# Keys and queries of one token tile as one unit of 1216 columns over three PSUM banks

## The chip, the cores and the metric

The kernel runs on one core of one Trainium2 chip. The metric is the device time of one execution in microseconds. A PSUM bank holds 512 fp32 columns for each of 128 partitions; the core has eight, numbered 0 to 7. The engines are TensorE (PE, with its weight loads as a lane of their own, PEld), VectorE (DVE), ScalarE (ACT), GpSimd (POOL) and SyncE (SP, which issues DMAs here).

## The reference

The input x has 2048 tokens of 640 features, in bf16. Two branches are mixed by a gate g = sigmoid(sum(x * gate_w)) per token:

```python
a = attention(x)                                   # 32 heads of 20
b = (gelu(x @ w_gate) * (x @ w_up)) @ w_down       # 1728 hidden columns
return g * a + (1 - g) * b
```

The attention is linear. With q, k, v = x @ wqkv, each head of q and k goes through a 20 x 20 matrix `w_phi`, and its features are softmax(p) and softmax(-p) side by side (40 of them). Then kv = phi_k^T v and z = sum of phi_k over all tokens, and each token gets phi_q kv / (phi_q z + 1e-6), followed by `@ wo`.

## The kernel before

Matmuls take a 128-token tile of x (transposed, `xT`, five blocks of 128 features) as the stationary operand and stream weights, so each projection of a tile is a group of five matmuls that accumulate in one bank, once for each feature block `kt`. Early on, `fold` multiplies `w_phi` into the K and Q weights and subtracts the last feature of each head, so that a head needs 19 columns: K and Q have 32 x 19 = 608 columns each, `wk2` inside the weight tile `w3` (beside V's 640 columns and the gate's one) and `wq2` in a tile of its own.

608 columns do not fit a bank. `k_tile` and `q_tile` each use a pair of banks and split the columns 304 and 304, so that the result lies contiguous over the border of the two banks: it begins at column `KO` = 208 of the first. `v_tile` does the same with 345 and 296 (`VO` = 167; 641 columns with the gate's). One ACT instruction then reads across the border: `exps` makes two of them for K or Q, exp(p) and exp(-p), into `Ek` or `Eqt`; V is copied into `vaug`. `exps` reads 33 heads in 11 groups of three, 627 columns, so the 19 columns behind the 608 must be zero; `strip` clears them in each second bank once. `gate_exp` handles the gate column (`gcol`), which comes with V, or with K for tiles 0 to 3 and 5.

The scheduler `_Sched` writes instructions in the program's order on each engine and tracks hazards by bank: a matmul into a bank waits for all that have read the bank before. The order is written out by hand in `attention_state`. K tiles 0 to 3 and V tiles 0 to 8 are done before the projection loop. The loop has 16 steps `s`, in turns of four by r = s % 4:

- r other than 1: `k_tile` of the next K tile (4 to 15) in banks 2 and 3, and `k_norm` on DVE (sums, reciprocal, scaling of `Ek`)
- s above 0 and r other than 0: `gram`, 11 matmuls (line 602) that add one K tile and its V to the state, which stays in banks 4 and 5
- s above 0 and r of 0 or 1: `v_tile` of the next V tile (9 to 15) in banks 0 and 1
- every step: `q_tile` of tile s in banks 6 and 7, and an SP transpose of `Eqt` into `Eq`
- every step above 0: one piece of the gate and up weights loaded on SP

Behind the loop `ffn` runs the gate and up projections (512-column matmuls), with the last four grams between them, then numerators (line 760) and the down and output projections (line 815).

All projections are recorded by the helper `mm` at line 459, so they share that line; shapes and operands tell them apart (`wq` is Q's weight before). `exps` is line 530, V's copy 500, the gate's exponential 520, the K normalisation lines 582, 590 and 591.

Of the kernel before, what the change touches and what calls it, by code (L numbers as in the profile page):

```python
# [3 lines left out]
P = 128  # L4
BF16 = mybir.dt.bfloat16
F32 = mybir.dt.float32
# [101 lines left out]
class _Kernel:  # L108
    S, D, H, DH, F = 2048, 640, 32, 20, 1728
    KD = D // P  # L110
# [16 lines left out]
    HG = 3  # L127
    UP = (4, 5, 6)
    LATE = (2, 3)
    VO = 167  # L130
    KO = 208

    def __init__(self, nc, A_x, A_wqkv, A_w_phi, A_wo, B_x, B_w_gate, B_w_up, B_w_down, gate_w, out):
        self.nc = nc
# [14 lines left out]
    def alloc(self):  # L149
        nc = self.nc  # L150
        S, D, KD, NT, BT, NFC, DH = self.S, self.D, self.KD, self.NT, self.BT, self.NFC, self.DH
        T = nc.alloc_sbuf_tensor
        self.xT = T("xT", [P, KD, S], BF16)
        self.wo_sb = T("wo_sb", [P, KD, D], BF16)
        self.wg_sb = T("wg_sb", [P, KD, 13 * P], BF16)
        self.wu_sb = T("wu_sb", [P, KD, 13 * P], BF16)
        self.wgu_sb = T("wgu_sb", [P, KD, P], BF16)
        self.wd_sb = T("wd_sb", [P, NFC, D], BF16)
        self.Eq = T("Eq", [P, self.G, S], BF16)
        self.KV = T("KV", [P, self.G, self.HG * self.DB], BF16)  # L160
        self.hmask = T("hmask", [P, 3, self.HG], BF16)
        self.mask = T("mask", [P, KD, 8], BF16)
        self.ident = T("ident", [P, P], BF16)
        self.gz = T("gz", [P, P], BF16)
        self.gcol = T("gcol", [P, NT], F32)
        self.gtmp = T("gtmp", [P, NT], F32)
        self.Gm = T("Gm", [P, NT], F32)
        self.Gr = T("Gr", [P, NT], F32)
        self.BD = T("BD", [P, KD, 8 * DH], BF16)
        self.wref = T("wref", [P, KD, self.H], F32)  # L170
        self.wphi_sb = T("wphi_sb", [P, KD, DH], BF16)

        def place(lists):
            size = {"b": 0}
            plans = []
            for items in lists:
                c = 0
                for name, shape, dt in items:
                    n = mybir.dt.size(dt)
                    for s_ in shape[1:]:  # L180
                        n *= s_
                    c = (c + 31) // 32 * 32
                    plans.append((name, shape, dt, c))
                    c += n
                size["b"] = max(size["b"], c)
            arena = T("arena%d" % len(self._arenas), [P, size["b"]], mybir.dt.uint8)
            self._arenas.append(arena)
            base = nc.lookup_mloc(arena).addr
            for name, shape, dt, c in plans:
                setattr(self, name, nc.alloc_sbuf_tensor_at(name, shape, dt, offset=base + c))  # L190
        self._arenas = []
        place([
            [("w3", [P, KD, D + 2 + self.H * self.E], BF16)],
            [("hT0", [P, NFC, BT], BF16), ("gl", [P, 3, BT], BF16)],
        ])
        place([
            [("Ek", [P, self.NSE, self.G * P], BF16), ("vaug", [P, self.NSV, self.H, self.DA], BF16)],
            [("hT1", [P, NFC, BT], BF16)],
        ])
        place([  # L200
            [("Eqt", [P, self.NEQ, self.G * P], BF16), ("Dk", [P, self.NSE, 2, 2 * self.G * self.HG], F32)],
            [("hT2", [P, NFC, BT], BF16)],
        ])
        place([
            [("wkT", [P, KD, D], BF16), ("wqT", [P, KD, D], BF16), ("wq2", [P, KD, self.H * self.E], BF16),
             ("xtok", [P, self.TB, D], BF16)],
            [("ahead", [P, 2 * KD, D], BF16), ("kstage", [P, self.HM * DH], F32)],
            [("upl", [P, len(self.LATE), BT], F32), ("qstage", [P, self.HM * DH], F32)],
            [("under", [P, KD, 2 * D + self.H * self.E], BF16), ("upf", [P, len(self.UP), BT], F32)],
            [("goT", [P, 8, KD, P], BF16), ("O1", [P, 2, D], BF16), ("O2", [P, 2, D], BF16),  # L210
             ("Og", [P, 2, D], BF16), ("RH", [P, 2, 8, self.H], F32), ("outsb", [P, 4, D], BF16)],
        ])
        self.ps = nc.alloc_psum_tensor("ps", [P, 4096], F32)
# [167 lines left out]
    def fold(self, name, main, tail, evacs, clear=None):  # L381
# [16 lines left out]
        for _, r, b, top, bot, (kt, i, k0, c, n) in sorted(order, key=lambda o: o[:2]):  # L398
            a, opens = 64 * r, opener.setdefault(b, r) == r
# [8 lines left out]
        for what, x in evacs:  # L408
            if what == "strip":
                self.strip(x)  # L410
            elif what == "tail":
                self.fold_evac(name, (0, 3)[x], (3, 2)[x], tail[x], self.HM, self.H)
            else:
                self.fold_evac(name, x, 1, main[x], 0, self.HM)

    def folded(self, name, kt, n, h0, w):
        T, c = (self.w3, self.D + 1) if name == "k" else (self.wq2, 0)
        c += h0 * self.E
        return T[:, kt:kt + n, c:c + w * self.E].rearrange("p k (h f) -> p k h f", f=self.E)

    def fold_evac(self, name, kt, n, b, h0, h1):
        w = h1 - h0
# [22 lines left out]
            dst, src[:, :, 0:self.E], src[:, :, self.E].unsqueeze(2).to_broadcast([P, self.HM, self.E]), ALU.subtract),  # L445
            reads=[key], writes=[("w%s2" % name, kt)])

    def strip(self, b, ek="d"):

        c = (b + 1) * 512 + 304  # L450
        dst, wr = self.ps[:, c:c + self.E], [("ps", b + 1)]
        if ek == "d":
            self.sc.op("dve", lambda e: e.memset(dst, 0.0), writes=wr)
        else:
            zero = self.nc.const_aps.tensor(0.0, [P, self.E], F32)
            self.sc.op("act", lambda e: e.activation(dst, zero, AF.Copy), writes=wr)
# [63 lines left out]
        self.sc.op("act", lambda e: e.activation(self.gcol[:, t:t + 1], self.ps[:, c:c + 1], AF.Exp, scale=-1.0),  # L520
                   reads=[("ps", b)], writes=[("gcol", t)])

    def exps(self, T, sl, name, b):

        o = b * 512 + self.KO
        src = self.ps[:, o:o + self.G * self.HG * self.E].rearrange("p (g h f) -> p g h f", h=self.HG, f=self.E)
        for s, scale in ((0, 1.0), (1, -1.0)):
            dst = T[:, sl, :].rearrange("p (g s w) -> p s g w", s=2, w=64)[:, s, :, 0:self.HG * self.DH].rearrange(
# [9 lines left out]
    def up_ahead(self, j, b, ek):  # L538
# [9 lines left out]
        else:  # L548
            self.sc.op("act", lambda e: e.activation(out, self.bank(b), AF.Copy), reads=[("ps", b)], writes=[("upf", c)],
                       guard=old)  # L550

    def k_tile(self, t, b):
        g = 1 if t < self.TB or t == 5 else 0
        n = 512 - self.KO + g
        self.proj(t, self.D + 1 - g, n, b, self.KO - g, ["wk2"] + ["wgate"] * g)
        self.proj(t, self.D + 1 - g + n, self.H * self.E + g - n, b + 1, 0, ["wk2", "wk2t"])
        self.exps(self.Ek, t % self.NSE, "Ek", b)
        if g:
            self.gate_exp(t, b, b * 512 + self.KO - 1)

    def q_tile(self, t, b):
        n = 512 - self.KO
        for bk, c0, a, z in ((b, self.KO, 0, n), (b + 1, 0, n, self.H * self.E)):
            for kt in range(self.KD):
                self.mm(bk, c0, z - a, self.xT[:, kt, t * P:(t + 1) * P], self.wq2[:, kt, a:z], kt == 0,
                        kt == self.KD - 1, [("xT", t), ("wq2", kt), ("wq2t", kt)])
        sl = t % self.NEQ
        self.exps(self.Eqt, sl, "Eqt", b)
        self.sc.dma("sp", lambda e: e.dma_start_transpose(self.Eq[:, :, t * P:(t + 1) * P], self.Eqt[:, sl, :]),
                    reads=[("Eqt", sl, 0), ("Eqt", sl, 1), ("Eqtc", sl), ("Eqtp", sl)], writes=[("Eq", t)])  # L570

    def k_view(self, se):
        v = self.Ek[:, se, :].rearrange("p (u w) -> p u w", w=64)[:, :, 0:self.HG * self.DH]
# [22 lines left out]
    def gram(self, t):  # L596
        se, sv = t % self.NSE, t % self.NSV
        w = self.HG * self.DA
        va = self.vaug[:, sv, :, :].rearrange("p h c -> p (h c)")
        for g in range(self.G):  # L600
            n, b, c = min(w, self.H * self.DA - w * g), 4 + g // 8, w * (g % 8)
            self.sc.op("pe", lambda e: e.matmul(  # L602
                self.bank(b)[:, c:c + n], self.Ek[:, se, g * P:(g + 1) * P], va[:, w * g:w * g + n],
                start=(t == 0 and g in (0, 8)), stop=(t == self.NT - 1 and g in (7, 10)), skip_group_check=True),
# [5 lines left out]
    def kv_state(self):  # L610

        sc = self.sc
        m = self.hmask[:, 2, :]
        for b, g0, n, h in ((4, 0, 8, 3), (5, 8, 2, 3), (5, 10, 1, 2)):
            c = (g0 % 8) * self.HG * self.DA
            src = self.bank(b)[:, c:c + n * h * self.DA].rearrange("p (g h c) -> p g h c", h=h, c=self.DA)
            dst = self.KV[:, g0:g0 + n, 0:h * self.DB].rearrange("p g (h c) -> p g h c", c=self.DB)[:, :, :, 0:self.DA]
# [17 lines left out]
    def attention_state(self):  # L635
# [20 lines left out]
        for t in range(4):  # L656
            vs(t, 4)
            ve([t], "ad"[t % 2], False)
            if t == 2:
# [13 lines left out]
        self.up_ahead(3, 0, "a")  # L673
        self.up_ahead(4, 2, "a")
        self.k_sums(0)
        self.fold("q", (4, 5, 0, 3, 1), (6, 7), [(m, 0), (m, 1), (p, 4), (m, 2), (m, 4), (p, 0), (t, 0), (t, 1), (p, 6)],
                  2)
        k(1, 2)
        k(2, 4)
        k(3, 0)  # L680
        v(8, 6)
        self.k_scale(0)
        for t in range(1, 4):
            self.k_norm(t)
        nk, nv, ng = 4, 9, 0
        pieces = self.gate_pieces()
        for s in range(NT):
            r = s % 4
            if r != 1:
                k(nk, 2)  # L690
                self.k_norm(nk)
                nk += 1
            if s and r != 0:
                self.gram(ng)
                ng += 1
            if s and r in (0, 1):
                v(nv, 0)
                nv += 1
            q(s, 6)
            if s:  # L700
                pieces.pop(0)()
        for p in pieces:
# [46 lines left out]
    def num(self, t):  # L749
        sc = self.sc  # L750
        NBK = self.NUMB
        DB, DH, H = self.DB, self.DH, self.H
        old = [("upf", c) for c in self.UP + self.LATE] + ["kstage", "qstage"] + [("wq2t", k) for k in range(5)] + [("xtok", k) for k in range(4)] + ["wkT", "wqT"] + [("wq2", k) for k in range(5)]
        w = self.HG * DB
        base = [(NBK + 2 * s) * 512 + 512 - 6 * w for s in (0, 1)]
        for g in range(self.G):
# [8 lines left out]
        sl = t % 2  # L765
# [28 lines left out]
    def down_pair(self, t0, banks, widths):  # L794
# [66 lines left out]
        (w, k) for w in ("vaug", "vmain", "vone") for k in range(9)]  # L861
    oldq = [("Eqt", k, s) for k in range(4) for s in (0, 1)] + [(w, k) for w in ("Eqtc", "Eqtp") for k in range(4)] + [
        (w, k) for w in ("Dk", "Rk") for k in range(5)]
    oldw = [(w, k) for w in ("wv", "wk2", "wk2t") for k in range(5)] + ["wgate"]

    def ffn(self):
        self.gn = 0
# [83 lines left out]
```

## Time and profile before

| | us |
|---|---|
| median of 3 runs | 283.37 (283.11 to 283.49) |
| profiled execution | 283.54 |
| its span in the profile | 282.3 |
| PE busy | 277.7 |
| DVE busy | 173.0 |
| ACT busy | 107.5 |
| granted TensorE clock | 1.00 |

Busy times are sums over the whole span. PE's rows overlap, since matmuls are pipelined, so the pace of matmuls is read from start to start.

### The profile page before, as it was taken

The page shows a single profiled execution, that of the slowest core. Times are in us where ns is not written, and L with a number is a line of the kernel's source. Part 1 is how long each engine was busy: PE and PEld are TensorE (multiplying, and loading weights), DVE is VectorE, ACT ScalarE, POOL GpSimd, SP SyncE. Part 2 cuts the span into 40 slices and gives each one's busy share as a digit, 9 for nine tenths or more (in the row PEclk, how much of TensorE's full clock was granted, in tenths as well). Part 3 has the DMA queues.
Part 4 walks back from the last instruction along what each step waited for, and adds up shares of the span by engine and source line. Part 5 has one row for each costly group of instructions (what it writes and reads, how often), then busy time and mean ns, then how long its engine had stood idle before and what let it go on. Part 6 is the DMA issues. An engine that isn't in the chain of part 4 may idle for free.

```text
span 282.3 us, 6982 instructions
## 1 busy us (share of the span) xinstructions
PE 277.7 (98%) x2958; PEld 172.8 (61%) x2972; DVE 173.0 (61%) x327; ACT 107.5 (38%) x203; POOL 15.2 (5%) x69
## 2 busy tenths in 40 slices
PE   7999999999999999999999999999999999999996
PEld 4576777777765444444444444445777777777786
DVE  1466999999997523666333324235883883883801
ACT  4347887878784332223232232321112112112011
POOL 7511010101100000000000000000000000000000
DMA  7999069878799910011000000000152152252221
GB/s 219 205 226 193 5 137 150 178 151 159 134 209 271 339 55 2 0 27 23 0 0 0 2 0 0 2 0 0 26 85 64 44 70 58 66 57 64 73 72 49
DMA packets 60234, 24.11 MB, mean 85 GB/s; under 512 B 50986, under 2 KB 59690, under 8 KB 60202
## 3 DMA queue, kind: packets, MB, share of 16 engines
q1 hardware_dynamic: 59536, 23.63, 38.7%
q8 instruction: 23, 0.38, 0.6%
q10 hardware_dynamic: 666, 0.03, 0.2%
q14 instruction: 9, 0.07, 0.1%
HBM read 9.04 MB, written 2.62 MB: 41 GB/s over the span
## 4 chain that ended last, share of the span: by engine, by line
PE 97%; DMA 1%; issue 0%; SPq 0%; ACT 0%
PE ps L459 62%; PE ps L815 29%; PE ps L760 2%; PE ps L471 2%; PE ps L602 2%; DMA w<-in_A_wqkv_dram 1%; PE ps L400 1%; SPq L230 0%; ACT outsb L828 0%; PE ps L366 0%
## 5 line engine op out<-in xcount | busy, mean ns | idle before, releaser
L459 PE MATMUL ps<-xT,wu_sb 128*128 128x512 bf16 x255 | 63.0, 379 | 0.4
L459 PE MATMUL ps<-xT,wg_sb 128*128 128x512 bf16 x251 | 62.0, 379 | 0.6 <-issue 0.3
L731 ACT ACTIVATE gl<-ps 128x512 bf16<-128x512 f32 x52 | 31.1, 597 | 70.5 <-PE ps L459 68.4
L815 PE MATMUL ps<-wd_sb,hT 64*128 64x320 bf16 x648 | 48.4, 296 | 0.0
L733 DVE TENSOR_TENSOR hT<-ps,gl 128x512 bf16<-128x512 f32 x34 | 23.2, 690 | 37.7 <-PE ps L459 37.7
L459 PEld LDWEIGHTS ps<-xT,wu_sb 128*128 128x128 bf16 x260 | 25.4, 98 | 30.4
L459 PEld LDWEIGHTS ps<-xT,wg_sb 128*128 128x128 bf16 x260 | 25.0, 98 | 29.4
L828 ACT ACTIVATE outsb<-ps,Gm 128x320 bf16<-128x320 f32 (+2 forms) x31 | 14.6, 516 | 71.8 <-PE ps L815 71.8
L459 PE MATMUL ps<-w,xT 128*128 128x304 bf16 (+5 forms) x280 | 40.2, 296 | 0.0
L815 PEld LDWEIGHTS ps<-wd_sb,hT 64*128 64x128 bf16 x648 | 30.9, 94 | 12.2 <-issue 0.4
L459 PEld LDWEIGHTS ps<-w,xT 128*128 128x128 bf16 x280 | 26.3, 97 | 10.5 <-ACT gcol L520 0.2
L815 PE MATMUL ps<-wo_sb,goT 64*128 64x320 bf16 (+2 forms) x340 | 26.5, 288 | 0.0
L582 DVE TENSOR_REDUCE Dk<-Ek 128x66 f32<-128x1320 bf16 x16 | 24.3, 1521 | 2.3 <-ACT gcol L520 2.3
L591 DVE TENSOR_TENSOR Ek<-Ek,Dk 128x1320 bf16<-128x1320 bf16 x16 | 24.5, 1533 | 0.5
L786 DVE TENSOR_TENSOR O<-ps,RH 128x640 bf16<-128x640 f32 x32 | 24.8, 816 | 0.0
L459 PE MATMUL ps<-wq,xT 128*128 128x304 bf16 x160 | 23.3, 292 | 0.0
L530 ACT ACTIVATE Eqt<-ps 128x627 bf16<-128x627 f32 x32 | 20.5, 693 | 6.4 <-PE ps L459 6.4
L530 ACT ACTIVATE Ek<-ps 128x627 bf16<-128x627 f32 x32 | 20.5, 693 | 1.9 <-PE ps L459 1.6
L733 DVE TENSOR_TENSOR xT<-ps,gl 128x512 bf16<-128x512 f32 x13 | 9.0, 692 | 18.2 <-PE ps L459 18.2
L815 PEld LDWEIGHTS ps<-wo_sb,goT 64*128 64x128 bf16 x340 | 15.9, 94 | 5.3
L459 PEld LDWEIGHTS ps<-wq,xT 128*128 128x128 bf16 x160 | 15.0, 97 | 4.5
L815 PE MATMUL ps<-wd_sb,xT 64*128 64x320 bf16 (+2 forms) x270 | 16.0, 269 | 0.0
(89 smaller groups left out, 184.1 us busy)
## 6 DMA issues: line engine op xcount, KB each, us to landing
out_dram<-outsb SPq DMA_DIRECT2D x7, 320.0 KB, 2.4
wd_sb<-in_B_w_down_dram SPq DMA_DIRECT2D x1, 2080.0 KB, 12.8
wg_sb<-in_B_w_gate_dram SPq DMA_DIRECT2D x5, 224.0 KB, 3.1
wg_sb<-in_B_w_gate_dram SPq DMA_DIRECT2D x5, 192.0 KB, 3.3
wu_sb<-in_B_w_up_dram SPq DMA_DIRECT2D x5, 192.0 KB, 4.6
w<-in_A_wqkv_dram SPq DMA_DIRECT2D x5, 160.0 KB, 4.0
wo_sb<-in_A_wo_dram SPq DMA_DIRECT2D x1, 800.0 KB, 10.6
xtok<-in_A_x_dram SPq DMA_DIRECT2D x2, 320.0 KB, 3.3
```

The lines of the kernel that those rows point to most:

```text
L459: self.sc.op("pe", lambda e: e.matmul(self.ps[:, bank * 512 + c0:bank * 512 + c0 + n], lhs, rhs, start=first, stop=fin), reads=reads, writ ...
L471: sc.op("pe", lambda e, c0=c0, n=n, bk=bk, col=col: e.matmul(self.bank(bk)[:, col:col + n], self.xT[:, kt, t * P:(t + 1) * P], self.w3[:, ...
L530: self.sc.op("act", lambda e: e.activation(dst, src, AF.Exp, scale=scale), reads=[("ps", b), ("ps", b + 1)], writes=[(name, sl, s)])
L582: self.sc.op("dve", lambda e: e.tensor_reduce(self.Dk[:, se, 0, :].rearrange("p (u h) -> p u h", h=self.HG), self.k_view(se), AX.X, ALU.ad ...
L591: sc.op("dve", lambda e: e.tensor_tensor(v, v, R.rearrange("p (u h) -> p u h", h=self.HG).unsqueeze(3).to_broadcast([P, 2 * self.G, self.H ...
L602: self.sc.op("pe", lambda e: e.matmul(self.bank(b)[:, c:c + n], self.Ek[:, se, g * P:(g + 1) * P], va[:, w * g:w * g + n], start=(t == 0 a ...
L731: sc.op("act", lambda e: e.activation(self.gl[:, slot, :], self.bank(banks[0]), AF.Gelu_apprx_tanh), reads=[("ps", banks[0])], writes=[("g ...
L733: sc.op("dve", lambda e: e.tensor_tensor(hT, up, self.gl[:, slot, :], ALU.mult), reads=[upk, ("gl", slot)], writes=[("hT", hk, c)], guard=old)
L760: sc.op("pe", lambda e: e.matmul(self.ps[:, o:o + n], self.Eq[a:a + 64, g, t * P:(t + 1) * P], self.KV[a:a + 64, g, 0:n], start=(g in (0, ...
L786: dve(lambda e, o=o, f=f, s=s: e.tensor_tensor(o, V[s][:, :, 0:DH], f, ALU.mult), rb + [key(6 + s)], [("O", s, sl)], guard=old)
L815: sc.op("pe", lambda e: e.matmul(self.bank(bk, w), lhs, rhs, start=opens and x == 0, stop=end and not opens, skip_group_check=True), reads ...
L828: sc.op("act", lambda e: e.activation(dst, self.bank(bk, w), AF.Copy, scale=g), reads=rd, writes=wr)
```

## The change

K and Q of tiles 4 to 15 become one unit in three banks, `kq_tile`: 362 columns of K in the first bank (from column 150), then one group of five matmuls of 492 columns that writes the remaining 246 of K to the start of the second bank and the first 246 of Q to its end (column 266 on), 20 columns apart, then 362 of Q in the third bank. That is 15 matmuls. Q's folded weights move into `w3` behind K's, so that the 492 columns lie side by side; its rows grow from 1250 to 1857 elements. K tiles 0 to 3 and Q tiles 0 to 3 stay alone, 362 + 246 or 246 + 362. V splits 395 and 246. Units, V tiles and Q tiles take banks 5 to 7 and 0 to 2 by turns, and the state lies in banks 3 and 4. In the loop, Q tiles 4 to 15 come with their K tiles, ahead of gram and V; Q tiles 0 to 3 come at the steps with r = 1.

The diff, cut to its core:

```diff
-    VO = 167
-    KO = 208
+    VO = 117
+    KN = 362
...
-            [("w3", [P, KD, D + 2 + self.H * self.E], BF16)],
+            [("w3", [P, KD, D + 1 + 2 * self.H * self.E], BF16)],
...
+                if x == 5:
+                    self.strip(6, c=self.KN)
...
-    def strip(self, b, ek="d"):
-
-        c = (b + 1) * 512 + 304
+    def strip(self, b, ek="d", c=None):
+
+        c = (b + 1) * 512 + (self.H * self.E - self.KN if c is None else c)
...
+    def k_gate(self, t):
+        return 1 if t < self.TB or t == 5 else 0
+
+    def k_first(self, t, b):
+        g, o = self.k_gate(t), 512 - self.KN
+        self.proj(t, self.D + 1 - g, self.KN + g, b, o - g, ["wk2"] + ["wgate"] * g)
+
+    def k_exps(self, t, b):
+        o = b * 512 + 512 - self.KN
+        self.exps(self.Ek, t % self.NSE, "Ek", o)
+        if self.k_gate(t):
+            self.gate_exp(t, b, o - 1)
...
+    def q_rest(self, t, b):
+        n, c = self.KN, self.D + 1 + 2 * self.H * self.E
+        self.proj(t, c - n, n, b + 2, 0, ["wq2", "wq2t"])
+        sl = self.nq % self.NEQ
+        self.nq += 1
+        self.exps(self.Eqt, sl, "Eqt", (b + 2) * 512 - (self.H * self.E - n))
         self.sc.dma("sp", lambda e: e.dma_start_transpose(self.Eq[:, :, t * P:(t + 1) * P], self.Eqt[:, sl, :]),
...
+    def q_tile(self, t, b):
+        n = self.H * self.E - self.KN
+        self.proj(t, self.D + 1 + self.H * self.E, n, b + 1, 512 - n, ["wq2", "wq2t"])
+        self.q_rest(t, b)
+
+    def kq_tile(self, t, b):
+        n = self.H * self.E - self.KN
+        self.k_first(t, b)
+        c, o, w = self.D + 1 + self.KN, (b + 1) * 512, 512 - n
+        out = self.ps[:, o:o + 2 * w].rearrange("p (r w) -> p r w", w=w)[:, :, 0:n]
+        for kt in range(self.KD):
+            sig = kt == self.KD - 1
+            self.sc.op("pe", lambda e: e.matmul(
+                out, self.xT[:, kt, t * P:(t + 1) * P], self.w3[:, kt, c:c + 2 * n].rearrange("p (r w) -> p r w", w=n),
+                start=kt == 0, stop=sig),
...
+        self.k_exps(t, b)
+        self.q_rest(t, b)
...
-            n, b, c = min(w, self.H * self.DA - w * g), 4 + g // 8, w * (g % 8)
+            n, b, c = min(w, self.H * self.DA - w * g), 3 + g // 8, w * (g % 8)
...
-        v(8, 6)
+        v(8, 2)
+        self.strip(1, "a", self.KN)
...
+        self.nq, self.half = 0, 1
+
+        def turn():
+            self.half ^= 1
+            return (5, 0)[self.half]
         for s in range(NT):
             r = s % 4
             if r != 1:
-                k(nk, 2)
+                self.kq_tile(nk, turn())
                 self.k_norm(nk)
                 nk += 1
             if s and r != 0:
                 self.gram(ng)
                 ng += 1
             if s and r in (0, 1):
-                v(nv, 0)
+                v(nv, turn())
                 nv += 1
-            q(s, 6)
+            if r == 1:
+                q(nq, turn())
+                nq += 1
             if s:
                 pieces.pop(0)()
```

What is left out keeps addresses and hazards in step: where `wq2` lay, fillers and the fold's reference column take its place, and the reuse of `w3` waits for Q's readers too.

More of the change, by code (lines that the diff above doesn't have):

```diff
@@ L169, in alloc @@
         self.BD = T("BD", [P, KD, 8 * DH], BF16)
-        self.wref = T("wref", [P, KD, self.H], F32)
         self.wphi_sb = T("wphi_sb", [P, KD, DH], BF16)
@@ L204, in alloc @@
         place([
-            [("wkT", [P, KD, D], BF16), ("wqT", [P, KD, D], BF16), ("wq2", [P, KD, self.H * self.E], BF16),
-             ("xtok", [P, self.TB, D], BF16)],
+            [("wkT", [P, KD, D], BF16), ("wqT", [P, KD, D], BF16), ("room", [P, 504], F32),
+             ("wref", [P, KD, self.H], F32), ("rest", [P, 856], F32), ("xtok", [P, self.TB, D], BF16)],
             [("ahead", [P, 2 * KD, D], BF16), ("kstage", [P, self.HM * DH], F32)],
@@ L416, in folded @@
     def folded(self, name, kt, n, h0, w):
-        T, c = (self.w3, self.D + 1) if name == "k" else (self.wq2, 0)
-        c += h0 * self.E
-        return T[:, kt:kt + n, c:c + w * self.E].rearrange("p k (h f) -> p k h f", f=self.E)
+        c = self.D + 1 + (h0 + (self.H if name == "q" else 0)) * self.E
+        return self.w3[:, kt:kt + n, c:c + w * self.E].rearrange("p k (h f) -> p k h f", f=self.E)
     def fold_evac(self, name, kt, n, b, h0, h1):
@@ L521, in gate_exp, with exps @@
                    reads=[("ps", b)], writes=[("gcol", t)])
-    def exps(self, T, sl, name, b):
-        o = b * 512 + self.KO
+    def exps(self, T, sl, name, o):
+        b = o // 512
         src = self.ps[:, o:o + self.G * self.HG * self.E].rearrange("p (g h f) -> p g h f", h=self.HG, f=self.E)
@@ L550, in up_ahead @@
                        guard=old)
-    def k_tile(self, t, b):
[L553 to L568, printed above, removed]
+    def k_gate(self, t):
+        return 1 if t < self.TB or t == 5 else 0
@@ new lines, in k_first @@
+    def k_first(self, t, b):
[6 more added lines that the diff above has]
+            self.gate_exp(t, b, o - 1)
+    def k_tile(self, t, b):
+        self.k_first(t, b)
+        self.proj(t, self.D + 1 + self.KN, self.H * self.E - self.KN, b + 1, 0, ["wk2", "wk2t"])
+        self.k_exps(t, b)
@@ new lines, in kq_tile @@
+    def kq_tile(self, t, b):
+        n = self.H * self.E - self.KN
+        self.k_first(t, b)
+        c, o, w = self.D + 1 + self.KN, (b + 1) * 512, 512 - n
[5 more added lines that the diff above has]
+                start=kt == 0, stop=sig),
+                reads=[("xT", t)] + [(k, kt) for k in ("wk2", "wk2t", "wq2", "wq2t")], writes=[("ps", b + 1)],
+                signal=sig)
+        self.k_exps(t, b)
+        self.q_rest(t, b)
@@ L613, in kv_state @@
         m = self.hmask[:, 2, :]
-        for b, g0, n, h in ((4, 0, 8, 3), (5, 8, 2, 3), (5, 10, 1, 2)):
+        for b, g0, n, h in ((3, 0, 8, 3), (4, 8, 2, 3), (4, 10, 1, 2)):
             c = (g0 % 8) * self.HG * self.DA
@@ L675, in attention_state @@
         self.k_sums(0)
-        self.fold("q", (4, 5, 0, 3, 1), (6, 7), [(m, 0), (m, 1), (p, 4), (m, 2), (m, 4), (p, 0), (t, 0), (t, 1), (p, 6)],
+        self.fold("q", (4, 5, 0, 3, 1), (6, 7), [(m, 0), (m, 1), (p, 4), (m, 2), (m, 4), (p, 0), (t, 0), (t, 1), (p, 5)],
                   2)
@@ L684, in attention_state @@
             self.k_norm(t)
-        nk, nv, ng = 4, 9, 0
+        nk, nv, ng, nq = 4, 9, 0, 0
+        self.nq, self.half = 0, 1
         pieces = self.gate_pieces()
+        def turn():
+            self.half ^= 1
+            return (5, 0)[self.half]
         for s in range(NT):
@@ L752, in num @@
         DB, DH, H = self.DB, self.DH, self.H
-        old = [("upf", c) for c in self.UP + self.LATE] + ["kstage", "qstage"] + [("wq2t", k) for k in range(5)] + [("xtok", k) for k in range(4)] + ["wkT", "wqT"] + [("wq2", k) for k in range(5)]
+        old = [("upf", c) for c in self.UP + self.LATE] + ["kstage", "qstage"] + [("wref", k, h) for k in (0, 3) for h in (0, self.HM)] + [("wref", k, 0) for k in (1, 2, 4)] + [("xtok", k) for k in range(4)] + ["wkT", "wqT"]
         w = self.HG * DB
@@ L863 @@
         (w, k) for w in ("Dk", "Rk") for k in range(5)]
-    oldw = [(w, k) for w in ("wv", "wk2", "wk2t") for k in range(5)] + ["wgate"]
+    oldw = [(w, k) for w in ("wv", "wk2", "wk2t", "wq2", "wq2t") for k in range(5)] + ["wgate"]
     def ffn(self):
```

## The prediction

> **What bounds the kernel now.** I read the page first (engines, chain), then the chain of waits in order of time, then the timeline of the one place where the change makes an engine late.
>
> ```profile
> span 282.3 us, 6982 instructions
> PE 277.7 (98%) x2958; PEld 172.8 (61%) x2972; DVE 173.0 (61%) x327; ACT 107.5 (38%) x203; POOL 15.2 (5%) x69
> ...
> PE 97%; DMA 1%; issue 0%; SPq 0%; ACT 0%
> PE ps L459 62%; PE ps L815 29%; PE ps L760 2%; PE ps L471 2%; PE ps L602 2%; DMA w<-in_A_wqkv_dram 1%; PE ps L400 1%; SPq L230 0%; ACT outsb L828 0%; PE ps L366 0%
> ```
>
> The chain that ended last is TensorE's own queue for 97% of the span. A microsecond given to or taken from PE's queue therefore arrives at the end whole, wherever it lies, and anything on another engine counts only when PE has to wait for it.
>
> The chain in order of time, over one turn of four steps of the projection loop and over one long run of 512-column matmuls:
>
> ```profile
> 41.01 0.33 PE ps L602 x11
> 41.34 5.26 PE ps L459 x40
> 46.60 0.33 PE ps L602 x11
> 46.93 3.96 PE ps L459 x30
> 50.90 0.33 PE ps L602 x11
> 51.23 2.60 PE ps L459 x20
> 53.83 0.34 PE ps L602 x11
> ...
> 158.08 10.74 PE ps L459 x49
> 168.82 0.05 issue
> 168.87 10.74 PE ps L459 x49
> ```
>
> Columns: start, length, engine and line, instructions. From 41.01 to 53.83 there is no piece that is not PE: the loop has no wait at all. The turn takes 12.82 us; the next two, from 53.83 and from 66.65, take 12.82 as well.
>
> **What a removed matmul is worth.** The turn has seven K or Q tiles (10 x 304 columns each) and two V tiles (5 x 345 and 5 x 296): 90 matmuls, 27,690 columns, in 12.82 - 3 x 0.33 = 11.83 us. The long run has 50 matmuls of 512 (one record is missing) in 10.79 us, 215.8 ns each. Two equations give 0.413 ns a column and 4.4 ns a matmul. A second reading, ten matmuls of 304 from 41.19 to 42.48 in the timeline (129 ns each), gives with the same long run 0.417 ns and 2.1 ns. I take the middle, 0.415 ns and 3.2 ns.
>
> The change merges two five-matmul groups into one in the twelve units of K tiles 4 to 15; K tiles 0 to 3 and Q tiles 0 to 3 keep ten matmuls each. That is 60 matmuls fewer and not one column fewer (362 + 492 + 362 = 4 x 304). Gain: 60 x 3.2 ns = 0.19 us (0.13 to 0.26). The removed weight loads count for nothing besides: the weight-load lane is idle for 3.1 us of each 12.82 us turn, and grams show a load and a matmul every 31 ns (0.34 us for 11).
>
> The Trainium skill, "TensorE: Matmul & The Clock Gate", section on the back-to-back issue gap, gives sustained 81 ns for 128 columns and 131 ns for 512. This trace has 215.8 ns for 512 and disagrees. By those figures each removed matmul would be worth 81 - 128 x 0.13 = 64 ns, an estimate from that page, and the change 3.9 us.
>
> **The merged matmul's output.** Its 492 columns go to two runs of 246 with 20 columns between them in one bank. No matmul of this trace writes two runs. Below zero I exclude: it streams as many columns. Lower end 0. Nearest row above: the 31 ns that a whole further weight load and matmul takes in a gram, 60 x 31 = 1.9 us. I take 0: the nearest rows are the projections themselves, which write 345 columns from an odd place (167), 296 from 0 and 304 from 208, all at one pace, so where a run begins costs nothing seen.
>
> The Trainium skill, "PSUM — Partial Sum Buffer", section Specifications (TRN2), says that any non-contiguous access pattern slows matmuls significantly. No row here shows it; were these 60 to run at half pace, that would be 60 x 0.21 = 12 us, an estimate.
>
> **The waits.** Before, K, Q and V tiles each had a bank pair of their own. Now a unit takes three banks, V and Q tiles share the two triples by turns, and a K/Q unit gives ScalarE four exponentials at once. The only place where that is late:
>
> ```profile
> 32.30 1.46 PE L459 MATMUL ps<-wq,xT 128*128 128x304 bf16 x10
> 32.56 1.28 ACT L530 ACTIVATE Ek<-ps 128x627 bf16<-128x627 f32 x2 [0.55 <-PE ps L459]
> ...
> 33.59 0.50 PE L602 MATMUL ps<-vaug,Ek 128*128 128x63 bf16 x11
> ...
> 33.85 1.28 ACT L530 ACTIVATE Eqt<-ps 128x627 bf16<-128x627 f32 x2
> ...
> 33.94 1.53 PE L459 MATMUL ps<-w,xT 128*128 128x345 bf16 x10
> ...
> 35.56 0.71 ACT L500 ACTIVATE vaug<-ps 128x640 bf16<-128x640 f32 x1 [0.43 <-PE ps L459]
> 36.16 0.17 ACT L520 ACTIVATE gcol<-ps 128x1 f32<-128x1 f32 x1
> ```
>
> Read from it: ScalarE starts 0.26 us after PE goes on to the next group (32.30 to 32.56); two pairs of exponentials take 35.13 - 32.56 = 2.57 us; a V copy with its gate column 0.77 us (35.56 to 36.33). PE restarts 0.05 us after a ScalarE release (at 39.48, to a matmul at 39.54).
>
> Step 0, tile 4's unit, begins where K tile 4 begins now, about 31.00. Groups of five: 362 columns 0.77 us, 492 columns 1.04, 362 columns 0.77. So K is complete at 32.81 and Q at 33.58; the K exponentials start at 33.07, Q's end at 35.64. PE meanwhile does gram 0 (to 33.92) and V 9 (to 35.28), then Q tile 0, whose first group goes into the bank that tile 4's K and Q both still hold. It can start at 35.69: **a new wait of 0.41 us**, since step 0 has no V tile. Everything behind it on PE (all later tiles, the gate and down projections) moves with it; ScalarE and SyncE's transpose for that Q tile move too.
>
> In later turns the same Q tile follows two V tiles. Counting from the unit's start: K exponentials 2.07, Q's end 4.64, first V copy and gate done 5.43 (it is ready at 3.94 but queues behind them), so PE may write at 5.48; with V (1.36), gram (0.34) and V again it arrives at 2.58 + 3.06 = 5.64. Margin 0.16 us, three times, at steps 5, 9, 13. The V tiles themselves need only banks released at 4.64 and earlier, by then 0.4 us or more before.
>
> One short wait goes: K tile 1's second half waits 0.03 us for a cleared strip on ScalarE (0.15 idle on the weight lane, but only 1.32 us against 1.29 for the tile); its longer first half now covers it.
>
> Edits at nothing: an extra clear on DVE (0.07 us) and one on ScalarE (0.19, in the 0.55 us idle before 32.56). DVE works through its K normalisations without pause until 85.80, and the last gram needs them at 88.43, 2.6 us cover. SyncE still issues one transpose and one weight load per step, tile 4's transpose first; the last piece of the gate and up weights is issued at 87.3, lands some 3 us later, and its first users start near 93. V's split 395 + 246 keeps its columns. K tiles 0 to 3 and V 8 find their banks free: V 8 starts at 29.62 and K tile 1's exponentials and gate end at 28.63. Longer rows of the weight tile put some at odd places, but fold results written at an odd column took 647 ns against 653 at an even one.
>
> **Sum.** -0.19 + 0.41 - 0.03 = +0.19 us. The profiled execution took 283.54 (span 282.3 and 1.24 around it), 0.17 over the median of 283.37. So 283.73 for such an execution, 283.6 for the median.
>
> **Rivals.** A measurement of this kernel can tell about 0.2%, 0.57 us, from no change.
>
> Slower, by the split output: it needs a cost per merged matmul above (0.57 - 0.19) / 60 = 6 ns; at 31 ns, +1.9, 285.4. For: no row shows a split output. Against: starts at odd columns are free. Since nothing here prices it, 0.26.
>
> Slower, by the thin margin: ScalarE late by 0.3 us or more in each turn (a unit now hands it four exponentials in a row, and 0.16 is little) makes the step-0 wait recur three times at up to 0.4: +1.2, 284.8. Against: its pairs take 1.28 everywhere. 0.16.
>
> Faster: a matmul would have to be worth (0.57 + 0.38) / 60 = 16 ns, or 10 ns without the step-0 wait; two readings say 2 to 4. About 282.5. 0.06.
>
> No new wait and the saving alone, 283.2, lies inside "same". That the change does not do what it says is true in part: 15 for 20 holds for 12 of 16 tiles, which the sum uses.
>
> Likeliest case, 0.52 together with 283.2: 283.2 to 283.9. The range leaves out faster (0.06) and the upper part of the slower rivals (about 0.14 of their 0.42: split outputs dearer than 27 ns, 60 x 27 ns = 1.6 us); 283.6 + 1.6 = 285.2 is its upper end, 283.0 its lower.
>
> **What would show it.** Turns of 12.77 to 12.78 us between grams in place of 12.82; one PE gap near 35.3 on a ScalarE exponential of about 0.4; no gap at steps 5, 9, 13; merged groups at 1.04 us per five. Wrong if a group of five takes over 1.07, or if turns are longer than 12.82.

## Result and the profile after

The changed kernel took 284.63 us (median of six runs, 284.13 to 284.75) beside 283.34 (283.11 to 283.77): a ratio of 1.0035, 95% interval 1.0023 to 1.0047. A second series on the chip gave 284.21 against 283.58, 1.0019 (1.0010 to 1.0029). It is slower, by 1.3 us in the first series and 0.6 in the second; against the 0.57 us that the prediction called the least it can tell, the first is clear and the second at the edge. The forecast of 283.6 lay 1.0 and 0.6 below; the range held both.

The page of the changed kernel, the lines that answer to those shown of before:

```profile
span 283.3 us, 6874 instructions
PE 279.6 (99%) x2912; PEld 168.1 (59%) x2912; DVE 173.0 (61%) x328; ACT 106.1 (37%) x204; POOL 15.2 (5%) x69
...
PE 96%; DMA 1%; ACT 1%; SPq 0%; issue 0%; ACTq 0%
```

PE still carries the chain, but ScalarE now has a percent of it. The chain in order of time shows where, and then one turn of four steps (line 591 is the merged group, 629 the gram):

```profile
33.51 1.28 ACT Ek L530 x2
34.79 1.18 ACT Eqt L530 x2
35.97 0.04 issue
36.02 2.24 PE ps L459 x15
...
43.00 0.33 PE ps L629 x11
43.33 0.78 PE ps L459 x5
44.10 1.04 PE ps L591 x5
45.15 2.13 PE ps L459 x15
47.28 0.33 PE ps L629 x11
...
55.79 0.33 PE ps L629 x11
```

The one wait stands where the prediction put it: the chain leaves PE for four exponentials and returns at 36.02, at Q tile 0. From there no piece is anything but PE, so the thin margin at steps 5, 9 and 13 held. A merged group takes 1.04 us, as reckoned. A turn takes 55.79 - 43.00 = 12.79 us for 12.82; 12.77 to 12.78 was forecast.

To see where the microsecond went, I cut the profiled execution of every kernel at the same places of the trace: the last fold matmul, the first matmul of the last gram, ScalarE's copy of the last output columns, and the end. All in us:

| kernel | span | to the last fold | folds to last gram | gram to last copy | tail |
|---|---|---|---|---|---|
| before | 282.29 | 25.59 | 62.84 | 191.78 | 2.08 |
| changed | 283.31 | 26.04 | 63.03 | 191.78 | 2.46 |
| changed, again | 282.78 | 25.59 | 63.03 | 191.78 | 2.38 |
| swap | 282.68 | 25.58 | 62.73 | 191.78 | 2.59 |
| align | 283.13 | 25.70 | 63.10 | 191.78 | 2.55 |
| shift | 282.16 | 25.27 | 63.03 | 191.78 | 2.08 |
| split | 282.66 | 25.64 | 63.16 | 191.78 | 2.08 |
| late | 284.52 | 27.52 | 62.84 | 191.78 | 2.38 |
| both | 282.13 | 25.53 | 62.73 | 191.78 | 2.09 |
| contig | 282.94 | 25.82 | 62.99 | 191.78 | 2.34 |

The stretch from the folds to the last gram (called the loop below), where nearly the whole edit lies, lost 0.19 us. The tail, in which not one instruction was edited, lost 0.30 to 0.38. The start, where only V's split, the place of Q's folded weights and one clear differ, lost 0.45 in the first profile and nothing in the second.

### The profile page after: what moved, and what is told of

It is laid out like the page before. It is cut to its first block, busy times and chain, and to the rows that moved or that the text cites. A ratio compares the mean times of both kernels' runs of the same rounds, so it can differ in the third digit from the quotient of the medians.

```text
span 283.3 us, 6874 instructions
## 1 busy us (share of the span) xinstructions
PE 279.6 (99%) x2912; PEld 168.1 (59%) x2912; DVE 173.0 (61%) x328; ACT 106.1 (37%) x204; POOL 15.2 (5%) x69
## 4 chain that ended last, share of the span: by engine, by line
PE 96%; DMA 1%; ACT 1%; SPq 0%; issue 0%; ACTq 0%
PE ps L459 57%; PE ps L850 28%; PE ps L591 4%; PE ps L471 2%; PE ps L795 2%; PE ps L629 2%; DMA w<-in_A_wqkv_dram 1%; PE ps L399 1%; ACT Ek L530 0%; ACT Eqt L530 0%; SPq L229 0%; ACT outsb L863 0%; PE ps L365 0%; ACTq L42 0%
## 5 line engine op out<-in xcount | busy, mean ns | idle before, releaser
L459 PE MATMUL ps<-xT,wu_sb 128*128 128x512 bf16 x260 | 64.1, 379 | 0.0
L459 PE MATMUL ps<-xT,wg_sb 128*128 128x512 bf16 x260 | 64.0, 379 | 0.0
L459 PE MATMUL ps<-w,xT 128*128 128x362 bf16 (+5 forms) x320 | 49.6, 304 | 0.1
L459 PEld LDWEIGHTS ps<-w,xT 128*128 128x128 bf16 x320 | 30.0, 97 | 15.2 <-ACT Eqt L530 0.4
L591 PE MATMUL ps<-w,xT 128*128 128x492 bf16 x60 | 14.5, 372 | 0.0
L810 DVE RECIPROCAL RH<-ps 128x32 f32<-128x32 f32 x16 | 5.7, 357 | 14.3 <-PE ps L795 14.3
```

The source lines that it names most:

```text
L459: self.sc.op("pe", lambda e: e.matmul(self.ps[:, bank * 512 + c0:bank * 512 + c0 + n], lhs, rhs, start=first, stop=fin), reads=reads, writ ...
L591: self.sc.op("pe", lambda e: e.matmul(out, self.xT[:, kt, t * P:(t + 1) * P], self.w3[:, kt, c:c + 2 * n].rearrange("p (r w) -> p r w", w= ...
L810: dve(lambda e: e.reciprocal(R(0), Dn[1]), rb, [key(0)], guard=old)
```

## Experiments

In the expectations, the times of the clock and of the instruction blocks, and the starts, count from 0.30 us ahead of the profile's zero: 6.77 is 6.47 in the profile, 280.67 is 280.37, and a start of 25.89 is 25.59.

**The changed kernel again.**

> The changed kernel unaltered, for its spread and a second profile. In the first profile it lost 1.0 us of span to the kernel before: 0.44 ahead of the first K tile's matmuls after the folds, 0.19 in the loop (the sum of the prediction), 0 from the last gram to the last matmul, 0.36 from the last matmul to the end. Theory 'clock': the 0.44 is the moment at which TensorE's clock comes to full speed (6.77 us in that profile, before 3.94 in the kernel before), which changes from run to run for either kernel: then it differs here by up to 0.5, and loop and tail do not. Theory 'layout': start and tail come from the moved addresses and stay as they are. Theory 'fetch': the tail stays at about +0.36. Ratio to before 1.002 to 1.005.

Measured 1.0019; start 25.59, folds to last gram 63.03, tail 2.38. The start's 0.45 is gone, loop and tail stayed. The rows of the start tell why (before, the changed kernel's first profile, its second; from 3 to 6 us; columns: line and operands, count, busy and mean ns):

```profile
L341 PE MATMUL ps<-ident,xtok 64*128 64x64 bf16 x40 | 0.9, 191 | 0.4 <-DMA xtok<-in_A_x_dram 0.3
```

```profile
L340 PE MATMUL ps<-ident,xtok 64*128 64x64 bf16 x40 | 1.5, 239 | 0.0
```

```profile
L340 PE MATMUL ps<-ident,xtok 64*128 64x64 bf16 x40 | 1.1, 208 | 0.0
```

The same transposes took 239 ns while the clock was not up and 191 once it was. The trace's clock record has full speed granted from 6.47 us in the first profile of the changed kernel and from 4.24 in the second; the profile of the kernel before has no such record. V's first matmul of 480 columns follows suit: it took 559 ns in the first profile and 363 in the second, with the next matmul 352 and 202 ns behind it (202 in the kernel before as well). It is one program with two starts: theory "clock" holds for what the two profiles show.

**The wait taken away.**

```diff
+            if s == 1:
+                q(nq, turn())
+                nq += 1
             if s and r in (0, 1):
                 v(nv, turn())
                 nv += 1
-            if r == 1:
+            if r == 1 and s > 1:
```

> Step 1 alone does Q tile 0 ahead of V tile 9, so that Q takes banks 1 and 2 and V banks 5 and 6. By the prediction's walk Q tile 0 then finds its banks released at about 32 us and V 9's second bank 0.5 us ahead of need: the one wait of 0.40 us goes and no other comes, the loop is 0.22 shorter than before instead of 0.19 longer, and the whole 0.40 us faster than the changed kernel. Rival: the wait only moves (V 9 or K/Q unit 5 waits for ScalarE as long), no gain.

Measured 284.00, 1.0015 (1.0006 to 1.0023); folds to last gram 62.73. The wait did not move, it went, and the loop is 0.30 us shorter than the changed kernel's, not 0.40. The total gained only 0.21 on the changed kernel's 284.21, and the profile's tail is 2.59, the longest of all, for 2.38. The chain now runs from gram 0 to the next unit on PE alone:

```profile
33.73 0.34 PE ps L629 x11
34.06 3.44 PE ps L459 x25
37.51 1.05 PE ps L591 x5
```

So the wait is worth 0.30, and without it the loop is 0.11 us shorter than before: that is all that the merge and the new order bring together.

**Rows and addresses as before.**

```diff
-            [("w3", [P, KD, D + 1 + 2 * self.H * self.E], BF16)],
+            [("w3", [P, KD, D + 2 + 2 * self.H * self.E], BF16), ("fill", [P, 16], BF16)],
```

> The weight tile's rows have 1858 elements for 1857 (all on 4-byte borders again), and a filler behind it puts all later tiles at 32 modulo 64 bytes, as in the kernel before. Theory 'layout': start and tail come back to before's, up to 0.8 us faster than the changed kernel. Theories 'clock' and 'fetch': no difference to the changed kernel beyond the clock's moment; the tail stays 0.36 longer than before.

Measured 284.19, 1.0024 (1.0015 to 1.0034); tail 2.55. The start (25.70) lies among those of the other profiles, and the tail did not come back: theory "layout" falls for the tail.

**The instruction blocks moved.**

```diff
-        for n in (512, 512, 512, 512, 512, 512, 128, 128, 128):
+        for n in (64,) * 48 + (128, 128, 128):
```

> The six warm-up matmuls of 512 columns ahead of everything become 48 of 64 (their results are used by nobody): 84 more TensorE instructions at the same number of columns. Theory 'fetch': in the changed kernel the last block of about 256 TensorE instructions is loaded at 280.67 us, 14 instructions from TensorE's end, while the last outputs are issued and written; with 84 more instructions behind the same count it comes about 2 us earlier, between two outputs, and the tail from the last matmul to the end is 2.1 us for 2.46: 0.36 faster. Theories 'layout' and 'clock': the tail stays at 2.46.

Measured 283.69, 0.9992 (0.9972 to 1.0011); tail 2.08, the value of before to the hundredth, folds to last gram unchanged at 63.03. Against the second profile of the changed kernel about 0.3 us of its gain is an earlier start (25.27 for 25.59), which the edit also touches; the other 0.30 is the tail, as theory "fetch" said.

**The merge alone undone.**

```diff
-        c, o, w = self.D + 1 + self.KN, (b + 1) * 512, 512 - n
-        out = self.ps[:, o:o + 2 * w].rearrange("p (r w) -> p r w", w=w)[:, :, 0:n]
-        for kt in range(self.KD):
...
+        c = self.D + 1 + self.KN
+        self.proj(t, c, n, b + 1, 0, ["wk2", "wk2t"])
+        self.proj(t, c + n, n, b + 1, 512 - n, ["wq2", "wq2t"])
```

> The changed kernel with the merge alone undone: in each of the twelve units the 492-column group becomes a group of 246 for K and one of 246 for Q at the same places, 20 matmuls for 15; banks, order and layout stay. Sum: 60 matmuls at 3.2 ns, the stretch from the folds to the last gram is 0.19 us longer than in the changed kernel (63.21 for 63.02). Theory 'fetch': these are 120 TensorE instructions more, the last block of instructions is loaded at about 278 again, and the tail is 2.06 for 2.4: together some 0.2 us faster than the changed kernel, although it does the merge's work in more matmuls. Without 'fetch': 0.19 slower than the changed kernel.

Measured 283.91, 1.0014 (1.0006 to 1.0023); folds to last gram 63.16, tail 2.08. The 60 matmuls cost 0.13 to 0.14 us, 2.3 ns each. And the kernel with more matmuls is not measurably slower than the merged one (1.0014 against 1.0019, intervals overlapping): in the profiles its loop is 0.13 us longer and its tail 0.30 shorter, since its 120 further instructions put the last block elsewhere (276.93 us).

**The kernel before, its last block made late.**

```diff
-        for n in (512, 512, 512, 512, 512, 512, 128, 128, 128):
+        for n in (32,) * 80:
```

> The kernel before with its nine warm-up matmuls made 80 of 32 columns (their results are used by nobody): 142 more TensorE instructions, so that the last block of instructions is due some 15 instructions ahead of TensorE's end, as in the changed kernel. Theory 'fetch': the tail is 2.4 to 2.5 us for 2.06; from the folds to the last gram 62.84 as before; the start may move by some tenths with the clock. Rival (the tail belongs to the changed kernel's layout or order): 2.06.

Measured 285.10, 1.0060 (1.0044 to 1.0076). Loop 62.84 as before, tail 2.38 for 2.08: the longer tail can be made in the kernel before, so it needs neither the change's layout nor its order. The DMA view of the last microseconds of this kernel (queues: packets, MB, share of the engines; issues: count, KB each, us to landing):

```profile
q8 instruction: 1, 0.02, 1.0%
issues: line engine op xcount, KB each, median us to landing
out_dram<-outsb SPq DMA_DIRECT2D x2, 128.0 KB, 2.1
out_dram<-outsb SPq DMA_DIRECT2D x1, 64.0 KB, 1.9
```

and the same view of "split", where no instruction block falls there:

```profile
q1 hardware_dynamic: 816, 0.33, 20.3%
issues: line engine op xcount, KB each, median us to landing
out_dram<-outsb SPq DMA_DIRECT2D x2, 128.0 KB, 1.8
out_dram<-outsb SPq DMA_DIRECT2D x1, 64.0 KB, 1.6
```

The rest of its loss is the start (27.52 for 25.59 in the profile): the shorter warm-up ended at 3.1 us, PE then stood idle for 0.85 us, and full speed was granted only at 9.41. This is one profile, and the edit changed the warm-up's length as well as its matmuls, so which of these put the clock off is not shown.

**Both costs removed.** The edits of "swap" and "shift" together.

> The changed kernel with Q tile 0 ahead of V tile 9 and 48 warm-up matmuls of 64 columns for six of 512: both costs gone. From the folds to the last gram 62.73 for 62.84 before, tail 2.06 as before, start 25.6 to 26.3 with the clock: 0.1 us faster than the kernel before, more if the shorter warm-up matmuls bring the start forward (25.57 for 25.89 in one run); 0.9 us faster than the changed kernel.

Measured 283.54 beside 283.53, 1.0002 (0.9993 to 1.0010). Folds to last gram 62.73, tail 2.09, start 25.53, all as expected. Against the changed kernel's second series it is 0.67 us better where 0.9 was expected, and from the kernel before it cannot be told apart. The 0.11 us of its loop is below what a measurement of the whole tells.

**The split output priced.**

```diff
-        out = self.ps[:, o:o + 2 * w].rearrange("p (r w) -> p r w", w=w)[:, :, 0:n]
+        out = self.ps[:, o + 512 - 2 * n:o + 512].rearrange("p (r w) -> p r w", w=n)
```

> The merged group writes its 492 columns side by side, at the end of the second bank, without the 20 columns between; K's last heads and Q's first are then read from shifted places, so the values are not the reference's. It prices the split output: theory 'free' 209 ns a matmul as in the changed kernel (209.3 from start to start); rival 'gap costs' up to the 207 ns or less that 492 columns take at the pace of the 512-column rows (0.415 ns a column and 3.2), 2 ns x 60 = 0.1 us.

From start to start 209.0 ns a matmul side by side, 209.3 with the gap (mean of 60 each): 0.3 ns, 0.02 us over all. The gap costs nothing that can be seen.

## Why the prediction was right or wrong

**What bounds the kernel: right up to the last output.** In the kernel before, PE's queue decides from 5.6 to 280 us; from the last gram to the last copy every kernel took 191.78. Behind that the output decides, and there the change lost time without any work of PE.

**What a removed matmul is worth: mis-sized.** I took 3.2 ns out of readings of 2.1 and 4.4; "split" against the changed kernel gives 0.13 to 0.14 / 60 = 2.3, and the gain 0.13 to 0.14 instead of 0.19. The low reading, ten equal matmuls in a row, was the good one. The equation over a whole turn took a gram as 0.33 us where it is 0.342 from its first matmul to that of the next group, and one pace for all columns where K's 304 took 130.0 ns and Q's 129.0; both went into the price of a matmul. In the loop as a whole 0.11 was left of the gain, since without the wait ("swap") it runs 62.73 for 62.84. The skill's sustained figures, which would have made it 3.9 us, do not hold here. In the Trainium skill, "TensorE: Matmul & The Clock Gate", the section on the back-to-back issue gap also has an isolated gap of N / 2.4 + 2.5 ns; its 2.5 agrees with the 2.3 here.

**The merged output: right.** No cost that can be seen (0.3 ns a matmul). The sentence of the Trainium skill, "PSUM — Partial Sum Buffer", Specifications (TRN2), that any non-contiguous pattern slows matmuls significantly does not hold for two runs of 246 columns here.

**The wait: right in place, mis-sized.** 0.41 was forecast, 0.30 is what removing it returned. I read two pairs of exponentials as 2.57 us from 32.56 to 35.13. But in the kernel before the second pair started at 33.85 because Q's matmuls ended at 33.59, 0.26 earlier: the row held a wait of its own. Back to back, as the changed kernel runs them, two pairs take 2.45 us:

```profile
33.51 1.28 ACT L530 ACTIVATE Ek<-ps 128x627 bf16<-128x627 f32 x2 [0.90 <-PE ps L591]
...
34.67 1.29 ACT L530 ACTIVATE Eqt<-ps 128x627 bf16<-128x627 f32 x2
...
36.01 1.87 PEld L459 LDWEIGHTS ps<-w,xT 128*128 128x128 bf16 x15 [0.40 <-ACT Eqt L530]
```

The second pair begins 0.12 us before the first has ended (34.67 for 34.79). The 0.40 of the last row is the weight lane's idle time, which includes the head start that a weight load usually has; it is not PE's loss. PE's own gap there is 0.39 us from one matmul's start to the next, where a matmul of 246 columns takes 0.105, which leaves 0.29 of waiting.

**The strip: not there.** The prediction let 0.03 us go with K tile 1's wait for the cleared strip. K tile 1 takes 1.32 us from start to start before and 1.31 after; K tiles without such a wait take 1.30 in the kernel before, not the 1.29 of a Q tile that it was compared with.

The errors, 0.11 too much wait and 0.11 too much gain (the strip's 0.03 among it), cancelled, and the sum of +0.19 met the loop's measured +0.19 by that luck.

**The step that failed: the removed weight loads "count for nothing besides".** The prediction priced only their time on the weight lane. That there are fewer instructions moved the places at which TensorE's instructions are loaded, a term that the sum did not have. By the packet times in the trace, the last block is loaded at 276.50 us in the kernel before, between two outputs; with 120 instructions fewer it comes at 280.37, when the last outputs leave. The end then comes 0.3 to 0.5 us later. Before, and the changed kernel, from 278 us on:

```profile
q1 hardware_dynamic: 816, 0.33, 20.0%
...
out_dram<-outsb SPq DMA_DIRECT2D x2, 128.0 KB, 1.8
out_dram<-outsb SPq DMA_DIRECT2D x1, 64.0 KB, 1.6
```

```profile
q8 instruction: 1, 0.02, 1.3%
...
out_dram<-outsb SPq DMA_DIRECT2D x2, 128.0 KB, 2.1
out_dram<-outsb SPq DMA_DIRECT2D x1, 64.0 KB, 2.0
```

One 16 KB packet of queue 8, and the last 64 KB take 0.4 us longer to land. The four kernels without that packet in the tail (before, shift, split, both) have 2.08 or 2.09 us, the six profiles with it 2.34 to 2.59. The other queue of instruction loads (q14) has its last packet some 14 us ahead of the last copy in every kernel. Loop 0.19 and tail 0.30 to 0.38 make 0.5 to 0.6 us, close to what the second series measured (0.63).

**The rivals.** Both series' medians lie on the side of "slower", but by neither mechanism that I gave: not the split output, and not the thin margin, which held at all three steps. A third one, instruction loading, was not on the list, so the chance of 0.42 for slower was better than its reasons.

**The first median.** 284.63 is 1.29 us above the kernel before, 0.7 more than loop and tail explain, and 0.4 above the second series. The first profile had its clock up late, which is worth 0.45; that the other runs of that series did too is not shown, since a profile sees one run. Two of the six, 284.13 and 284.16, lie at the second series' level. Left open as well is how the packet delays the output: the outputs' issue on SyncE's queue is longer too (1.62 us for 1.24 over the last two), and no run separates a shared DMA engine from a later issue.

## What to carry to other kernels

A row's duration read off between two engines may hold a wait; before it goes into a sum, look for the same pair of instructions where nothing keeps them apart. Where instructions are added or removed by the hundred, look at the queue of instruction loads and where its last packets fall against the first and last transfers of data: a gain of 0.13 us was lost there more than twice over. And cut the trace at fixed landmarks: with loop, start and tail apart (the loop came out at 63.03 in three profiles), 0.1 us can be read from a single profile that the total, with a spread of half a microsecond, can't resolve.

## What the runs showed of the hardware

TensorE's instructions arrive in packets of 16 KB on queue 8 (23 of them, 0.38 MB, in either kernel), on average 255 to 257 of its recorded instructions apart. The last one falls 14 such instructions ahead of TensorE's end in the changed kernel, 102 in "shift" with 84 more instructions and 158 in "split" with 120 more. One that falls on the last output costs 0.3 to 0.5 us; from the last gram to the last copy the packets fall at other places in each kernel, and all take 191.78. The Trainium skill, "Runtime: NRT & Kernel Launch", section on instruction fetch mechanics, has blocks of 16 KiB or 256 instructions and calls the cost mostly hidden; size, spacing and that stretch agree, but on the last output it showed.

The moment at which the clock comes to full speed differed between two profiles of one program by 2.2 us (4.24 and 6.47), worth 0.45 us; in the one profile of "late", whose warm-up ended 0.85 us before the first data, it came at 9.41, with a start 1.9 us longer. The Trainium skill, "TensorE: Matmul & The Clock Gate", Part 1, describes a free-running window of 3.4 us whose place varies from run to run; a difference of 2.2 us fits within one such window, though it is more than the 500 ns either way that the page gives.
